# Turning the scaled keys in 32x32 blocks on VectorE and placing the blocks by DMA, in place of transposes on TensorE

## The chip, the core and the metric

The kernel runs on one core of a Trainium2 chip. A core has a matrix engine (TensorE, "PE" in the profile, with its weight loads as "PEld"), three elementwise engines (VectorE "DVE", ScalarE "ACT", GpSimd "POOL"), a queue engine that here does nothing but issue DMA transfers (SyncE, "SP"), and 16 DMA engines that move the data. Each engine runs its own instructions in the order in which they stand in the program; engines wait for one another only by semaphores. The metric is the device time of one execution in microseconds: before the change 647.9 us, the median of three runs (647.87 to 648.56).

## The reference

```python
def _attn_ref(r, k, v, w, u):                    # batch 4, heads 8, tokens 768, head size 48
    for t in range(S):
        cur = einsum('bhd,bhe->bhde', u * k[t], v[t])
        y[t] = einsum('bhd,bhde->bhe', r[t], state + cur)
        state = w[t] * state + einsum('bhd,bhe->bhde', k[t], v[t])

x = attn_out.transpose(0, 2, 1, 3).reshape(3072, 384)
h = x @ w_in                                     # 384 x 2048
out = (h * sigmoid(h)) @ w_out                   # 2048 x 384
```

A recurrence with a 48x48 state for each head and batch, whose rows decay by w at every token, and after it a two-layer network with SiLU between the layers. All is float32.

## The kernel before

**Units.** The work is cut in 12 units. A unit is one block of 128 tokens (six of them, n = 0 to 5) for two of the four batches, so unit i has n = i // 2. Units 0 and 1 take another path through the transposes (`i < NTOK`), and units 2 to 11 are alike. Of the two batches of a unit the second (b = 1) is kept with its tokens in reverse.

**Inside a unit.** Decays, queries and keys lie with channels on the partitions: `tw`, `tr` and `tk` hold for partition 64*e + d channel d of the even or odd head e of a pair, and along the free dimension rows of 128 tokens, one row for each head pair (NP = 4) and batch. Seven levels (l = 0 to 6) then build the scores of queries against keys in blocks of 1, 2, 4 ... 64 tokens. At each level TensorE makes the score products (line 527), VectorE keeps what the mask of the level allows (`keep_level`, line 537) and scales the queries (`grow_queries`, line 473, `prepare`, line 595), GpSimd scales the keys (`grow_keys`, line 491), and ScalarE copies. `burst` makes two levels of products in one go. `bonus_spread` and `bonus_write` (lines 440 to 452) put the term of u on the diagonal of the scores.

After level 6 the keys in `tk[:, NP:3*NP]` are scaled for the new state. The output is `y_state` (line 652, queries times the old state) plus `y` (line 665, scores times values), and `update` (line 679) adds keys times values to the decayed state. For `update` tokens have to lie on the partitions, since it sums over tokens; that is what `turn_k` is for: eight TensorE transposes of 128x128 (line 639, four for each batch) into PSUM, and a ScalarE copy of each batch's result to the tile `kq` (line 640). Units 10 and 11 hold the last tokens, and `update` returns at once for them (line 674), while `turn_k` is called for them too. `tk` has 16 rows: rows 4 to 11 are the keys, and rows 0 to 3 and 12 to 15 (`X = 0, NP + Q`) are scratch for the levels.

**The network.** `up(i, m)` (line 757, SiLU on line 763) makes a slice of the first layer for a whole unit, `quarter(i, x)` (line 820) seven products that give the second layer, with sums on VectorE (lines 802 and 829). Both lag behind the attention: while unit i is in its attention part, `quarter` of unit i - 2 and `up` of unit i - 1 are slipped in.

**What sets the order.** Nothing reorders the program (`manual_schedule`); it is written out by hand. For units 3 to 11 the loop at line 920 takes the groups of `mix(i)` one by one and puts after each of them the number of network steps that `ROOM` gives. Unit 2 is written out at lines 909 to 917. So on TensorE `turn_k` stands between two network steps near the unit's end, and `y_state`, `y` and `update` come after the last step of the unit, with the quarters of the next unit behind them.

**The DMA queue.** All loads and stores of units 2 to 11 are issued on SyncE's queue, in program order: per unit 48 loads of blocks of w, k and r for the unit after next (`load_blocks`, line 106, each 32 partitions x 8 rows x 32 or 16 values), five of v (lines 119 and 126), four of r and k for the bonus term (line 90), four that move the bonus sums (line 425), ten that move `yt` to `xt` (`move_x`, line 715) and two stores of the output (line 833).

Of the kernel before, what the change touches and what calls it, by code (L numbers as in the profile page):

```python
# [8 lines left out]
F32 = mybir.dt.float32  # L9
# [29 lines left out]
def kernel(  # L39
# [11 lines left out]
    nc = tc.nc  # L51

    B, H, S, D = r.shape
# [3 lines left out]
    NB = 2  # L57
    NP = H // 2
    PD = 64
    Q = NB * NP  # L60
    NX = Q + 2 * NP
    X = 0, NP + Q
# [3 lines left out]
    units = [(n, b0) for n in range(S // L) for b0 in range(0, B, NB)]  # L66
    NSLOT = 2
    NTOK = 2
# [4 lines left out]
    pt = ctx.enter_context(tc.tile_pool(name="pt", bufs=2))  # L73
    ps = ctx.enter_context(tc.tile_pool(name="ps", bufs=1, space=bass.MemoryType.PSUM))
# [174 lines left out]
    ident = const.tile([128, 128], F32, name="ident")  # L249
# [72 lines left out]
    tw, tr, tk, diag, kq, xt = {}, {}, {}, {}, {}, {}  # L322
# [297 lines left out]
    apart = {}  # L620
# [8 lines left out]
                                    ident[rows, rows])  # L629

    def turn_k(i, b):
        kq[i, b] = pt.tile([128, NP, 2 * PD], F32, name="kq")
        if i < NTOK:
            for e, have in enumerate(apart[i]):
                nc.scalar.copy(out=kq[i, b][:, :, PD * e:PD * e + D], in_=have[:, b])
            return
        p_tr = ps.tile([128, NP, 2 * PD], F32, name="p_m", bufs=2)
        for p in range(NP):
            nc.tensor.transpose(p_tr[:, p, :], tk[i][:, NP + (p, 2 * NP - 1 - p)[b], :], ident)  # L639
        nc.scalar.copy(out=kq[i, b], in_=p_tr)  # L640

    p_yt, p_kv, yt = {}, {}, {}

    def values(i, b):
        return vq[i] if b == 1 else vt[i]
# [25 lines left out]
    def update(i, b):  # L671
        n, b0 = units[i]
        if n == S // L - 1:
            return
        if b == 0:
            p_kv[i] = ps.tile([128, NB, NP, D], F32, name="p_m" if i < NTOK else "p_sc", bufs=2)
        for p in range(NP):
            for e in range(2):
                nc.tensor.matmul(p_kv[i][PD * e:PD * e + D, b, p, :], lhsT=kq[i, b][:, p, PD * e:PD * e + D],  # L679
                                 rhs=values(i, b)[:, 2 * p + e, :], start=(b == 0 and p == 0),  # L680
                                 stop=(b == NB - 1 and p == NP - 1))
        new = state[:, b0 + b]
        if n > 0:
            nc.gpsimd.tensor_tensor(out=new, in0=new,  # L684
                                    in1=tw[i][NL][:, b * NP:(b + 1) * NP, :].to_broadcast([128, NP, 2 * PD]),
                                    op=ALU.mult)
        if b < NB - 1:
            return
        for e in range(2):
            rows, cols = slice(PD * e, PD * e + D), slice(PD * e, PD * e + D)  # L690
            new = state[rows, b0:b0 + NB, :, cols]
            if n > 0:
                nc.vector.tensor_tensor(out=new, in0=p_kv[i][rows], in1=new, op=ALU.add)
            else:
                (nc.scalar.copy if i == 0 else nc.vector.tensor_copy)(out=new, in_=p_kv[i][rows])
# [23 lines left out]
    def both(fn, i, *args):  # L719
        return [(fn, i, b, *args) for b in range(NB)]  # L720

    def block_loads(i):
        return [(load_blocks, i, name, g) for name in "wkr" for g in range(4)]

    def mix(i):

        groups = [[*both(turn, i, "w"), (product, i, 0)],
                  [*both(turn, i, "k"), *both(turn, i, "r"), (odd_ones, i)], [(start_levels, i), (prepare_keys, i, 1)],
                  [(prepare, i, 1), *[(product, i, l) for l in range(1, NL)]],
                  [(burst, i, 1), (keep_level, i, 1)], [(keep_level, i, 2), (go_on, i, 2)],  # L730
                  [(prepare, i, 3), (reverse_v, i), (bonus, i, 0)],
                  [(burst, i, 3), (keep_level, i, 3), (bonus_sum, i, 0), (bonus, i, 1), (bonus, i, 2)],
                  [(keep_level, i, 4), (go_on, i, 4)],
                  [(prepare, i, 5), (bonus_sum, i, 1)] + ([(load_rk, i + 1)] if i + 1 < len(units) else []),
                  [(burst, i, 5), (keep_level, i, 5)], [(keep_level, i, 6), (go_on, i, 6), (bonus_spread, i), (bonus_write, i)],
                  both(turn_k, i), [*both(y_state, i), *both(y, i), *both(update, i), (move_x, i)]]

        loads = block_loads(i + NSLOT) if i + NSLOT < len(units) else []
        if i + 1 < len(units):
            loads.insert(len(loads) // 2, (load_values, i + 1))  # L740

        behind = groups[3 if i > NTOK + 1 else 10:]
        for at, group in enumerate(behind):
            group += loads[at * len(loads) // len(behind):(at + 1) * len(loads) // len(behind)]
        return groups
# [101 lines left out]
    def do(*steps):  # L847
        for fn, *args in steps:
            fn(*args)
# [20 lines left out]
    for l in range(1, NL):  # L870
        do((scores, 0, l), *[(grow_keys, 0, l + 1)] * (l + 1 < NL), *others[l])

    do((bonus, 1, 0), (bonus, 1, 1), (bonus, 1, 2), *both(y, 0), (turn_apart, 0), (join_weight, 0), (add_weight,),
       (product, 1, 0), (tail_weight, 1), (turn, 1, 0, "k"), (join_weight, 1), (dense_x, 0, 0), (turn, 1, 1, "k"),
       (dense_x, 0, 1), (grow_queries, 1, 0), (odd_ones, 1), (tail_weight, 2), *both(turn_k, 0), (head_weight, 2),
       (start_keys, 1, nc.gpsimd, True), (add_weight,), (up, 0, 0), (join_weight, 2), *blocks[4:8],
       (start_keys, 1, nc.gpsimd, False), (add_weight,), (tail_weight, 3), (odd_keys, 1, 1), (head_weight, 3), (grow_keys, 1, 1),
       (scores, 1, 1, (join_weight, 3)), (add_weight,), (up, 0, 1), (tail_weight, 4), (grow_keys, 1, 2), (head_weight, 4),
       (up, 0, 2))


    others = {1: blocks[8:12], 2: [(bonus_sum, 1, 0), (bonus_sum, 1, 1), (load_rk, 2), *both(update, 0)],
              3: [(bonus_spread, 1), (reverse_v, 1), (clear, 1), (load_values, 2)]}

# [4 lines left out]
    for m in range(1, 4):  # L889
# [3 lines left out]

    do((scores, 1, NL - 1), (join_weight, 8), (add_weight,), (up, 0, 7), *both(y, 1), (turn_apart, 1),
       (tail_weight, 9), *both(turn_k, 1), (dense_x, 1, 0), (head_weight, 9, [0]), (dense_x, 1, 1), (head_weight, 9, [1]),
       (join_weight, 9), (add_weight,), (tail_weight, 10), (head_weight, 10), *both(update, 1), (up, 1, 0), *both(turn, 2, "w"))
    blocks = block_loads(3)

# [5 lines left out]
    for m in range(6):  # L904
# [7 lines left out]
    do(blocks[2], (burst, 2, 3), (keep_level, 2, 3), (keep_level, 2, 4), (go_on, 2, 4), (prepare, 2, 5), (bonus, 2, 1),  # L912
       (bonus, 2, 2), (down, 0, 1, 2), (bonus_sum, 2, 1), (load_rk, 3), (sums, 1, 1), *blocks[3:7], (down, 0, 1, 3))
    do((burst, 2, 5), (keep_level, 2, 5), (keep_level, 2, 6), (go_on, 2, 6), (up, 1, 6), (bonus_spread, 2), (bonus_write, 2),
       (load_values, 3), *both(turn_k, 2), (weight_sums, 2), (up, 1, 7), (sums, 1, 2))
    do((sums, 1, 3), *both(y_state, 2), *both(y, 2), *both(update, 2), (move_x, 2),
       *blocks[7:])

    ROOM = 1, 1, 0, 2, 1, 1, 1, 1, 1, 2, 1, 2, 1, 0
    for i in range(3, len(units)):  # L920
        steps = downs(i - 2) + ups(i - 1)
        groups = mix(i)
        if i == NTOK + 1:

            groups[4].insert(1, (weight_sums, 3))
        for group, room in zip(groups, ROOM):
            do(*group)
            for step in steps[:room]:
                do(*step)
            steps = steps[room:]  # L930
# [32 lines left out]
```

## Time and profile before

| what | before |
|---|---|
| time, median of 3 | 647.9 us |
| span of the profiled run | 646.2 us |
| TensorE busy | 639.6 us |
| VectorE busy | 433.9 us |
| GpSimd busy | 283.1 us |
| ScalarE busy | 203.8 us |
| mean DMA rate | 76 GB/s |
| granted TensorE clock, mean | 1.000 |
| `turn_k`: transposes on line 639 | 80, 0.87 us for each eight on the chain |
| `turn_k`: copies on line 640 | 20, median 581 ns |

The busy times say how much an engine has to do in all. What sets the time is the chain of work that ended last: the profile follows it back from the last instruction, at each step to what released it. Of one unit in the middle of the run the engines' timelines and SyncE's own list of DMA issues tell how far each engine is ahead of the chain. In that list a transfer stands with the time that its issue occupied the queue; the time from issue to landing stands apart.

### The profile page before, as it was taken

How to read it: one execution, taken by the hardware profiler on the slowest of the kernel's cores; microseconds unless marked ns; L12 is line 12 of the kernel's file. 1: busy time of each engine (PE TensorE's matmuls, PEld its weight loads, DVE VectorE, ACT ScalarE, POOL GpSimd, SP SyncE). 2: the span in 40 equal slices, each digit the busy share in tenths (PEclk: the TensorE clock that was granted, in tenths of full speed). 3: DMA queues.
4: the chain of work that ended last, by engine and by line, in shares of the span. 5: the costliest groups of instructions: out<-in, count | busy, mean ns of one | idle time of the engine just before them, and what ended most of it. 6: DMA issues, size and time to landing. Idle time of an engine off the chain costs nothing.

```text
span 646.2 us, 12889 instructions
## 1 busy us (share of the span) xinstructions
PE 639.6 (99%) x4878; PEld 579.2 (90%) x4878; DVE 433.9 (67%) x737; ACT 203.8 (32%) x408; POOL 283.1 (44%) x356
## 2 busy tenths in 40 slices
PE   8999999999999999999999999999999999999998
PEld 7888876898899899899899899899899989989997
DVE  7879789896777677586586586676586766751031
ACT  5798872212321321320321231231232232131120
POOL 6898398466065054254334425416416505510000
PEclk9999999999999999999999999999999999999999
DMA  9975954433534524513513513423432022000000
GB/s 229 276 180 131 229 129 50 91 75 52 96 63 69 96 49 72 88 31 64 98 29 67 96 28 58 96 37 52 90 54 38 26 50 50 27 2 25 25 0 25
DMA packets 201134, 49.21 MB, mean 76 GB/s; under 512 B 188912, under 2 KB 195952, under 8 KB 201072
## 3 DMA queue, kind: packets, MB, share of 16 engines
q1 hardware_dynamic: 199488, 47.79, 36.5%
q10 hardware_dynamic: 1584, 0.59, 0.4%
q8 instruction: 39, 0.64, 0.4%
q14 instruction: 23, 0.19, 0.1%
HBM read 39.52 MB, written 4.72 MB: 68 GB/s over the span
## 4 chain that ended last, share of the span: by engine, by line
PE 95%; DVE 2%; POOL 1%; ACT 1%; issue 1%; POOLq 0%; DVEq 0%; ACTq 0%
PE p_h L757 39%; PE p_o L820 31%; PE p_sc L527 6%; PE p_m L527 4%; PE p_m L776 3%; PE p_m L665 3%; PE p_m L652 3%; PE p_m L639 1%; PE p_sc L679 1%; POOL tk L491 1%; PE p_m L350 1%; PE p_m L855 1%; PE p_m L703 0%; DVE score L450 0%; POOL w_in_sb L227 0%
## 5 line engine op out<-in xcount | busy, mean ns | idle before, releaser
L757 PE MATMUL p_h<-xt,w_in_sb 128*128 128x256 f32 x1152 | 258.4, 382 | 0.7 <-POOL tk L507 0.7
L757 PEld LDWEIGHTS p_h<-xt,w_in_sb 128*128 128x128 f32 x1152 | 215.8, 190 | 32.5 <-POOL tk L507 0.9
L763 ACT ACTIVATE gt<-p_h 128x512 f32<-128x512 f32 x93 | 55.5, 596 | 228.2 <-PE p_h L757 228.1
L491 POOL TENSOR_TENSOR tk<-tk,tw 128x256 f32<-128x256 f32 x144 | 102.1, 732 | 23.3 <-ACT tk L461 16.6
L537 DVE COPY_PREDICATED score<-mask,p_sc 128x512 f32<-128x512 int8 x78 | 64.1, 885 | 59.7 <-PE p_sc L527 59.4
L820 PE MATMUL p_o<-own,temps 128*128 128x192 f32 x528 | 90.3, 328 | 0.4 <-DVE temps L829 0.4
L820 PE MATMUL p_o<-w_out_sb,gt 128*128 128x192 f32 x528 | 90.4, 328 | 0.0
L820 PEld LDWEIGHTS p_o<-own,temps 128*128 128x128 f32 x528 | 85.8, 190 | 1.8 <-DVE temps L829 0.7
L820 PEld LDWEIGHTS p_o<-w_out_sb,gt 128*128 128x128 f32 x528 | 85.9, 190 | 0.9 <-issue 0.4
L684 POOL TENSOR_TENSOR state<-state,tw 128x512 f32<-128x512 f32 x16 | 19.3, 1225 | 118.5 <-PE p_m L652 118.5
L386 POOL TENSOR_TENSOR tw<-tw 128x256 f32<-128x256 f32 (+6 forms) x83 | 39.8, 480 | 54.5 <-DVE tw L338 50.6
L802 DVE TENSOR_TENSOR temps<-gt 128x256 f32<-128x256 f32 x88 | 44.3, 504 | 21.9 <-ACT gt L763 21.9
L461 ACT COPY tk<-tk 128x256 f32<-128x256 f32 x60 | 24.6, 410 | 83.4 <-PE p_sc L527 40.8
L527 PEld LDWEIGHTS p_sc<-tr,tk 48*128 48x128 f32 x640 | 39.2, 186 | 12.1 <-issue 8.9
L473 DVE TENSOR_TENSOR tr<-tr,tw 128x512 f32<-128x512 f32 x53 | 46.0, 868 | 3.3 <-POOL tk L491 1.0
L527 PE MATMUL p_sc<-tr,tk 48*128 48x128 f32 x640 | 47.1, 285 | 0.6 <-POOL tk L491 0.6
L408 POOL TENSOR_TENSOR ruk<-tokens_rk 128x768 f32<-128x768 f32 x10 | 18.6, 1858 | 65.8 <-DVE own_sums L415 65.8
L595 DVE TENSOR_TENSOR tr<-tr,tw 128x512 f32<-128x512 f32 x29 | 39.9, 1375 | 1.3
L537 DVE COPY_PREDICATED score<-mask,p_m 128x512 f32<-128x512 int8 x54 | 35.4, 706 | 0.0
L820 PE MATMUL p_o<-w_out_sb,temps 128*128 128x192 f32 x176 | 30.4, 326 | 0.0
L829 DVE TENSOR_TENSOR partial<-p_o,partial 128x192 f32<-128x192 f32 x33 | 11.6, 353 | 27.6 <-PE p_o L820 27.6
L597 ACT COPY tr<-tr 128x512 f32<-128x512 f32 x29 | 18.4, 634 | 35.8 <-DVE tr L473 35.0
(144 smaller groups left out, 753.3 us busy)
## 6 DMA issues: line engine op xcount, KB each, us to landing
w_out_sb<-in_moe_w_in_dram SPq DMA_DIRECT2D x6, 768.0 KB, 6.9
tokens_rk<-in_r_dram SPq DMA_DIRECT2D x20, 192.0 KB, 3.4
tokens_rk<-in_k_dram SPq DMA_DIRECT2D x20, 192.0 KB, 3.8
w_out_sb<-in_moe_w_out_dram SPq DMA_DIRECT2D x4, 768.0 KB, 6.3
own<-in_moe_w_out_dram SPq DMA_DIRECT2D x4, 768.0 KB, 5.8
xt<-yt SPq DMA_DIRECT2D x60, 48.0 KB, 2.0
raw<-in_w_dram SPq DMA_DIRECT2D x80, 32.0 KB, 2.2
raw<-in_k_dram SPq DMA_DIRECT2D x80, 32.0 KB, 2.4
```

Of the source, the lines that this page charges most:

```text
L386: engine.tensor_tensor(out=up, in0=t[:, :, 0::2], in1=t[:, :, 1::2], op=ALU.mult)
L461: nc.scalar.copy(out=keys(i, X[(l + 1) % 2] * L + c, [4 * c, blocks], [c, 2], [1, c]), in_=keys(i, NP * L + c, [4 * c, blocks], [NP * L + ...
L473: nc.vector.tensor_tensor(out=odd, in0=odd, in1=tw[i][l][:, :, 0::2][:, :, :, None].to_broadcast([128, Q, L >> (l + 1), c]), op=ALU.mult)
L491: nc.gpsimd.tensor_tensor(out=out, in0=have, in1=odd_products(i, l, b, *blocks), op=ALU.mult)
L527: nc.tensor.matmul(bass.AP(tensor=s_p.tensor, offset=s_p.offset, ap=[s_p.ap[0], [apart * L // 2, 2], [1, L // 2]]), lhsT=tk[i][rows, X[l % ...
L537: nc.vector.copy_predicated(out=dst, mask=masks[l][:, :, None].to_broadcast([128, NB, NP, ni, c]), data=sc[e].rearrange("p (b q) (i c) -> ...
L595: nc.vector.tensor_tensor(out=new[:, :, :, 1, :], in0=old[:, :, :, 1, :], in1=tw[i][l][:, :, 0::2][:, :, :, None].to_broadcast([128, Q, L ...
L652: nc.tensor.matmul(p_yt[i, b][:, p, :], lhsT=state[:, b0 + b, p, :], rhs=tr[i][:, b * NP + p, :], start=(p == 0), stop=False)
L757: nc.tensor.matmul(p_h[:, a, :], lhsT=w_in_sb[:, c, f * 128:(f + 1) * 128], rhs=xt[i][:, c, :], start=(c == 0), stop=(c == KC - 1))
L763: nc.scalar.activation(out=gt[i, m], in_=p_h, func=AF.Silu)
L802: nc.vector.tensor_tensor(out=out, in0=one, in1=two, op=op)
L820: nc.tensor.matmul(p, lhsT=left(f), rhs=right[:, f, :], start=(f == 0), stop=(f == FH - 1))
```

## The change

The transposes leave TensorE. For units 2 to 9 `turn_blocks` has VectorE turn the scaled keys in blocks of 32x32, one instruction of 128x512 for each batch, into the scratch rows of `tk`; a block then lies on the partitions of its channels, and its place in `kq` is on the partitions of its tokens. So 32 DMA transfers (2 halves of a head's channels x 2 heads of a pair x 4 groups of tokens x 2 batches) move the blocks to `kq`. `kq` becomes one tile for both batches, with one buffer. Units 10 and 11 turn no keys. Units 0 and 1 keep their path, with the new shape of `kq`. In `mix` the group with `turn_k` falls away, `turn_blocks` goes to the end of the group before it, and `ROOM` gives this group the three network steps of both.

```diff
     def turn_k(i, b):
-        kq[i, b] = pt.tile([128, NP, 2 * PD], F32, name="kq")
-        if i < NTOK:
-            for e, have in enumerate(apart[i]):
-                nc.scalar.copy(out=kq[i, b][:, :, PD * e:PD * e + D], in_=have[:, b])
-            return
-        p_tr = ps.tile([128, NP, 2 * PD], F32, name="p_m", bufs=2)
-        for p in range(NP):
-            nc.tensor.transpose(p_tr[:, p, :], tk[i][:, NP + (p, 2 * NP - 1 - p)[b], :], ident)
-        nc.scalar.copy(out=kq[i, b], in_=p_tr)
+        if b == 0:
+            kq[i] = pt.tile([128, NB, NP, 2 * PD], F32, name="kq", bufs=1)
+        for e, have in enumerate(apart[i]):
+            nc.scalar.copy(out=kq[i][:, b, :, PD * e:PD * e + D], in_=have[:, b])
+
+    def turn_blocks(i):
+
+        kq[i] = pt.tile([128, NB, NP, 2 * PD], F32, name="kq", bufs=1)
+        for b in range(NB):
+            nc.vector.transpose(out=tk[i][:, X[b]:X[b] + NP, :], in_=tk[i][:, NP + b * NP:2 * NP + b * NP, :])
+        for a in range(2):
+            width = min(D - 32 * a, 32)
+            for e in range(2):
+                t = tk[i][(2 * e + a) * 32:(2 * e + a + 1) * 32]
+                for g in range(4):
+                    for b in range(NB):
+                        nc.sync.dma_start(out=kq[i][g * 32:(g + 1) * 32, b, :, PD * e + 32 * a:PD * e + 32 * a + width],
+                                          in_=t[:, X[b]:X[b] + NP, g * 32:g * 32 + width])
...
+        back = b == 1 and i >= NTOK
         for p in range(NP):
             for e in range(2):
-                nc.tensor.matmul(p_kv[i][PD * e:PD * e + D, b, p, :], lhsT=kq[i, b][:, p, PD * e:PD * e + D],
+                nc.tensor.matmul(p_kv[i][PD * e:PD * e + D, b, p, :], lhsT=kq[i][:, b, NP - 1 - p if back else p, PD * e:PD * e + D],
...
-                  [(burst, i, 5), (keep_level, i, 5)], [(keep_level, i, 6), (go_on, i, 6), (bonus_spread, i), (bonus_write, i)],
-                  both(turn_k, i), [*both(y_state, i), *both(y, i), *both(update, i), (move_x, i)]]
+                  [(burst, i, 5), (keep_level, i, 5)],
+                  [(keep_level, i, 6), (go_on, i, 6), (bonus_spread, i), (bonus_write, i), *[(turn_blocks, i)] * (i < len(units) - NB)],
+                  [*both(y_state, i), *both(y, i), *both(update, i), (move_x, i)]]
...
-       (load_values, 3), *both(turn_k, 2), (weight_sums, 2), (up, 1, 7), (sums, 1, 2))
+       (load_values, 3), (turn_blocks, 2), (weight_sums, 2), (up, 1, 7), (sums, 1, 2))
...
-    ROOM = 1, 1, 0, 2, 1, 1, 1, 1, 1, 2, 1, 2, 1, 0
+    ROOM = 1, 1, 0, 2, 1, 1, 1, 1, 1, 2, 1, 3, 0
```

## The prediction

> **What bounds the kernel now.** I read the page's first part, then the chain that ended last in order of time, cut to one unit (unit 6), then VectorE's timeline and SyncE's issues over the same microseconds.
>
> ```profile
> PE 639.6 (99%) x4878; PEld 579.2 (90%) x4878; DVE 433.9 (67%) x737; ACT 203.8 (32%) x408; POOL 283.1 (44%) x356
> ```
>
> TensorE is busy for all but 1% of the span. The chain (start, us, engine, tile and line) shows that it is also what everything ends on: start follows start without a gap.
>
> ```profile
> 315.75 0.89 PE p_m L527 x16
> 316.64 7.97 PE p_h L757 x36
> 324.61 0.87 PE p_m L639 x8
> 325.48 2.59 PE p_h L757 x12
> 328.07 1.78 PE p_m L652 x16
> 329.86 1.88 PE p_m L665 x32
> 331.74 0.72 PE p_sc L679 x32
> 332.46 10.60 PE p_o L820 x64
> ...
> 366.69 0.89 PE p_m L527 x16
> 367.58 7.97 PE p_h L757 x36
> ```
>
> The last products of scores end at 316.64; call this moment E. The eight transposes take 0.87 us of the chain, and `update` (L679) begins at E + 15.10. From its end at 332.46 to the next unit's E at 367.58 are 35.12 us, and a unit takes 50.94.
>
> VectorE's timeline tells when the new turning could begin: the last write of scores ends at 323.75, E + 7.1. The turning of the raw keys, the same instruction and shape, takes 669 ns.
>
> ```profile
> 321.25 2.50 DVE L450 COPY_PREDICATED score<-own_mask,both_b 128x1024 f32<-128x1024 int8 x2
> ...
> L338 DVE STREAM_TRANSPOSE tk<-raw x20: 667/669/705, 78.8 to 535.8; 128x512 f32<-128x512 f32 x20
> ```
>
> SyncE's issues (start, us, line, transfer, count) are the view that decides. Eight loads of blocks take 3.90 us of the queue, 0.49 each, whether a run is 128 or 64 bytes; ten moves from SBUF to SBUF 6.29, 0.63 each, and four of the smaller ones 2.44, 0.61 each.
>
> ```profile
> 310.75 2.44 SPq L425 DMA_DIRECT2D diag<-own_sums  x4
> ...
> 320.17 3.90 SPq L106 DMA_DIRECT2D raw<-in_r_dram  x8
> 332.40 6.29 SPq L715 DMA_DIRECT2D xt<-yt  x10
> ```
>
> The page gives 2.0 us from issue to landing for such a move:
>
> ```profile
> xt<-yt SPq DMA_DIRECT2D x60, 48.0 KB, 2.0
> ```
>
> **What the Trainium skill says.** "Perfetto Trace Analysis", section What "DMA-bound" means, counts as one of its bounds the issuing engine's sequencer when its track is solid DMA slices, since that window is descriptor generation and not data movement. The trace agrees: the issues lie end to end at a fixed price, while the DMA engines are busy 36% in this unit (windows view).
>
> "VectorE: DVE Perf Modes", section The three transpose paths: VectorE turns blocks of 32x32 only, not a full 128x128. So the blocks must be carried to other partitions, which is what the 32 transfers are; the trace confirms the price of the turning alone.
>
> "TensorE: Matmul & The Clock Gate", section Part 1: after an idle window of about 3.4 us the array runs at half rate until it has been busy about as long. The record of the granted clock shows 1.00 throughout, but the warming matmuls agree: the first sixteen took 3.68 us, sixteen of the same a little later 1.97.
>
> ```profile
> 1.36 3.68 PE L855 MATMUL p_m<-ident 128*128 128x128 f32 x16 [1.36 <-POOL ident masks.py:199]
> ...
> 11.70 1.97 PE L855 MATMUL p_m<-ident 128*128 128x128 f32 x16
> ```
>
> **Removed.** Eight transposes in each of ten units: 10 x 0.87 = 8.7 us of the chain. Twenty ScalarE copies of 581 ns: ScalarE is busy 32% and waits for TensorE, so nothing. With the two last units nothing comes in their place, so there 2 x 0.87 = 1.7 us is a clear gain.
>
> **Added on VectorE.** Two turnings a unit, 2 x 0.67 = 1.34 us, from E + 7.1 to E + 8.45. Behind them stand the sums of line 802, which the second layer needs about 10 us later, in its third product, and VectorE is busy 35 of the 50.94 us. GpSimd has scaled the keys long before, since its queue is idle from 313.2. Nothing for VectorE, then, except as the start of what follows.
>
> **Added on SyncE.** 32 transfers a unit. No row shows exactly this shape, so I bound it: below by the block loads, 0.49 us (also 32 partitions and three dimensions, but from HBM), above by a little over the moves to `xt`, 0.65. I take 0.61, the small SBUF moves, because these also begin and end in SBUF. That the DMA engines keep up is seen at 316 to 324: 16 loads, 4096 packets of at most 128 bytes, at a busy share of 0.61 (windows view), and 32 blocks are again 4096 packets, over more than twice the time.
>
> The first transfer waits for the first turning, the second for the second, at E + 8.45. The thirty after it come at 0.61: the last is issued at E + 8.45 + 18.3 = E + 26.75 and lands 2.0 later, at E + 28.75.
>
> **The new wait.** `update` sums over all tokens, so each of its matmuls needs all four token groups and both halves of the channels of its head: the first batch's set ends with the next to last transfer. On TensorE `update` stands before the next unit's quarters, and the engine keeps order. Without the transposes it would be reached at E + 15.10 - 0.87 = E + 14.2. So TensorE stands still for 28.75 - 14.2 = 14.5 us, and `update` comes 28.75 - 15.10 = 13.65 us later than before. Nothing gives this back: the state, the next turning of w, k and r on VectorE and the quarters all stand behind it. With 0.49 and a landing of 2.2 (the block loads) it is 8.45 + 14.7 + 2.2 - 15.10 = 10.25; with 0.65 and 2.5, 15.35.
>
> **Unit 2 is worse off,** since there SyncE is already late:
>
> ```profile
> 132.64 2.15 SPq L126 DMA_DIRECT2D vq<-in_v_dram  x4
> 134.90 6.56 SPq L715 DMA_DIRECT2D xt<-yt  x10
> ```
>
> Its transfers come after these loads of v and ahead of the moves to `xt`, so at 134.9, though the blocks would be turned at about 126. The last lands at 134.9 + 31 x 0.61 + 2.0 = 155.8; `update` of unit 2 began at 127.2. That is 28.6 us (24.9 to 30.4).
>
> **Does the queue keep up later?** In a steady unit 73 other issues (48 loads x 0.49, ten xt x 0.63, the rest) are some 38 us of queue between the last block of one unit and the first of the next. From that last block's issue to the next turned keys TensorE needs 2.0 + 0.72 + 35.12 + 1.7 + 8.45 = 48 us. It keeps up. Only before unit 4 are there 98 issues (loads of unit 3 move behind its blocks), 51 us: 3 us more.
>
> **Cold clock.** Each of the eight stalls is far over 3.4 us. I take 3.68 - 1.97 = 1.7 us each from the start of the trace, 13.6 in all; ends 0 and 3.4 (two windows lost at half rate).
>
> **Sum.** 28.6 + 7 x 13.65 + 3 + 13.6 - 1.7 = 139.0. Forecast: 647.9 + 139 = 787 us.
>
> **Rivals.**
> *The placing is hidden, and the transposes are a gain.* For: before, SyncE is idle from 324.07 to 332.40, just where the blocks come, and TensorE is the bound. Against: hiding 32 issues before E + 14.2 allows (14.2 - 2.0 - 8.45) / 30 = 0.125 us each, and no transfer in SyncE's list comes near. It would give 647.9 - 8.7 = 639 us.
> *The stall is there but short,* because an SBUF block issues in 0.31 us, the least that any block load took. Then a steady unit is 8.45 + 9.3 + 2.0 - 15.10 = 4.65 later, unit 2 134.9 + 9.6 + 2.0 - 127.2 = 19.3; with 13.6 for the clock and 1.7 off: 647.9 + 7 x 4.65 + 19.3 + 13.6 - 1.7 = 712 us. Against: the median of the loads is 449 ns, and no move between SBUF tiles went under 522.
> *SyncE becomes the bound outright,* if a block costs over 0.9 us by a slow path for its three dimensions: each unit then adds 8.45 + 27 + 2.0 - 15.1 = 22.4, and unit 2 37.6: 647.9 + 7 x 22.4 + 37.6 + 13.6 - 1.7 = 854 us. Nothing in the profile speaks for it but that the shape is new.
>
> **How the numbers follow.** Forecast 0.78, hidden 0.05, short stall 0.11, slow path 0.06. The ends of the forecast: 24.9 + 7 x 10.25 + 3 - 1.7 = 98, so 746 with no cold clock; 30.4 + 7 x 15.35 + 3 + 27.2 - 1.7 = 166, so 814. To have 8 in 10 I go a little towards the short stall and past the top: 737 to 820. Faster is the hidden case alone, 0.05; for a result within 0.2% a stall would have to cancel the gain to a microsecond, 0.01; slower 0.94.
>
> **What would show it.** In the profile after: TensorE idle for about 14 us a unit ahead of the `update` matmuls, eight times, the first about twice as long, released by the DMA of `kq`; 32 issues of `kq` in a row on SyncE, about 0.6 us apart, the first right after VectorE's turnings of 0.67 us; a unit period near 66 us, against 50 for the last two; matmuls at double time for some microseconds after each stall. Wrong it would be if the issues come closer together than 0.4 us, or if matmuls after the stall keep their speed.

## The result, and the profile after

After the change the kernel takes 804.5 us (median of four runs, 803.0 to 805.45) against 648.1 us before on the same chip (647.87 to 648.56): the ratio is 1.241, with an interval of 1.2395 to 1.243. The change costs 156.4 us. The forecast was 787 us, with a range of 737 to 820.

The first part of the page after has TensorE busy for only 82% of the span of 802.4 us. In the second part the clock row now has gaps, where it showed full speed throughout before. The fourth part, the chain, has SyncE's queue as the second largest holder.

```profile
PE 655.4 (82%) x4798; PEld 591.3 (74%) x4798; DVE 439.1 (55%) x753; ACT 193.8 (24%) x388; POOL 285.2 (36%) x356
...
PEclk9999997599779959987995997899699699999999
...
PE 72%; SPq 17%; DVE 3%; POOL 2%; issue 2%; DMA 2%; ACT 1%; POOLq 0%; ACTq 0%
```

The same two rows before:

```profile
PEclk9999999999999999999999999999999999999999
...
PE 95%; DVE 2%; POOL 1%; ACT 1%; issue 1%; POOLq 0%; DVEq 0%; ACTq 0%
```

The chain of unit 6, in order of time (start, us, what), answers to the one shown of before. E, the end of the last products of scores, is 405.71 here.

```profile
405.71 7.98 PE p_h L768 x36
413.71 0.61 ACT gt L774
414.32 0.54 SPq L648
...
433.21 0.59 SPq L648
...
433.85 1.77 DMA kq<-tk
...
435.76 1.49 PE p_sc L689 x30
437.25 12.14 PE p_o L831 x64
449.39 1.11 PE p_sc L527 x16
```

Before, the chain ran through TensorE from E to `update` without leaving it. Now it leaves TensorE at E + 8, goes through SyncE's queue one issue at a time for 19.5 us, and comes back at 435.76, E + 30.05. What follows is slower as well: `update` takes 1.49 us instead of 0.72, and the first quarters take 12.14 us instead of 10.60.

SyncE's list and TensorE's timeline over the same microseconds show both sides of the wait. The brackets hold the idle time before an instruction and what ended it.

```profile
413.44 21.65 SPq L648 DMA_DIRECT2D kq<-tk  x32
```

```profile
430.62 0.36 PE L689 MATMUL p_sc<-vt,kq 128*48 128x48 f32 x2 [10.69 <-DMA kq<-tk]
435.76 0.77 PE L689 MATMUL p_sc<-vt,kq 128*48 128x48 f32 x13 [4.77 <-DMA kq<-tk]
```

32 issues follow one another for 21.65 us, 0.68 each. TensorE stands still from 419.9 (430.62 - 10.69) to 435.76, but for two matmuls of an even head, whose blocks are issued ahead of the odd head's and have all landed.

The table of stretches gives the granted clock of the same stall. Its columns are the stretch, its length, then busy time and count of TensorE, of its weight loads, of VectorE, ScalarE and GpSimd, then the clock, the DMA share and GB/s.

```profile
421.00:425.00 4.00, 0.00 (x0) 0.00 (x0) 0.54 (x2) 0.00 (x0) 0.00 (x0) 0.78 0.16 24
425.00:429.00 4.00, 0.00 (x0) 0.00 (x0) 0.00 (x0) 0.00 (x0) 0.00 (x0) 0.50 0.13 15
...
435.70:439.70 4.00, 3.94 (x38) 3.88 (x39) 2.32 (x4) 0.00 (x0) 0.00 (x0) 0.50 0.31 53
439.70:443.70 4.00, 4.00 (x25) 4.00 (x24) 2.47 (x5) 0.98 (x2) 3.27 (x5) 0.92 0.19 49
```

A mean of 0.78 over four microseconds is 2.2 us at full speed and then half, so the clock fell at about 423.2, 3.3 us into the stall. It came back at about 440.3, 4.6 us after work had begun again. Over the eight stalls the trace's clock record has the fall 2.6 to 3.8 us into the stall and the return 3.2 to 5.3 us after the work. All changes in this record lie whole multiples of 3.41 us apart, so each of these times also depends on how the stall lies to these steps. While the blocks are being placed, hardly anything is computed and the DMA engines are busy 0.13 to 0.16: nothing is short of bandwidth.

The 156.4 us can be put together from the start times of `update` in the two chains:

| part | later than before, us | forecast, us |
|---|---|---|
| unit 2 (127.34 before, 155.59 after) | 28.3 | 28.6 |
| units 3 and 5 to 9, growth of each over its period before | 16.8, 16.1, 17.2, 16.6, 17.3, 17.4: sum 101.4 | 6 x 15.35 = 92.1 |
| unit 4 | 25.6 | 15.35 + 3 = 18.35 |
| after the last `update`: its cold clock, less the transposes of the two last units | 0.9, the rest of the spans' difference of 156.2 | 1.7 - 1.7 = 0 |
| sum | 156.2 | 139.0 |

(15.35 is the forecast's 13.65 for the stall and 1.7 for the clock.)

Unit 4 is the one that doesn't follow the others. SyncE's list (it ends at 285, so it has ten of the 32), ScalarE's timeline and TensorE's timeline before its stall:

```profile
267.11 2.44 SPq L425 DMA_DIRECT2D diag<-own_sums  x4
...
276.54 1.93 SPq L106 DMA_DIRECT2D raw<-in_r_dram  x4
278.56 6.64 SPq L648 DMA_DIRECT2D kq<-tk  x10
```

```profile
269.53 0.20 ACT L441 COPY both_b<-diag 128x16 f32<-128x16 f32 x1 [3.83 <-DMA diag<-own_sums]
```

```profile
272.17 4.54 PE L768 MATMUL p_h<-xt,w_in_sb 128*128 128x256 f32 x12 [1.93 <-ACT gt L774]
```

E of this unit is 262.3. SyncE reaches the blocks at E + 16.3, where it was at E + 7.7 in unit 6. The 98 issues since the blocks of unit 3 took it from 223.4 to 278.6, 55.2 us, and it waited for nothing in between. The moves of the bonus sums, which stand in the same queue, are late as well: ScalarE waits 3.83 us for them before its SiLU, and TensorE 1.93 us for ScalarE. This second stall, ahead of the first, adds nothing to the time here: VectorE's turnings end at 275.6, SyncE comes to the blocks only at 278.6, straight from its loads, and `update` begins when they have landed, at 300.6. The whole delay of unit 4 is the queue's.

### The profile page after: what moved, and what is told of

Same layout as the page of the kernel before. It is cut to its first block, busy times and chain, and to the rows that moved or that the text cites. A ratio compares the mean times of both kernels' runs of the same rounds, so it can differ in the third digit from the quotient of the medians.

```text
span 802.4 us, 13027 instructions
## 1 busy us (share of the span) xinstructions
PE 655.4 (82%) x4798; PEld 591.3 (74%) x4798; DVE 439.1 (55%) x753; ACT 193.8 (24%) x388; POOL 285.2 (36%) x356
## 4 chain that ended last, share of the span: by engine, by line
PE 72%; SPq 17%; DVE 3%; POOL 2%; issue 2%; DMA 2%; ACT 1%; POOLq 0%; ACTq 0%
PE p_h L768 30%; PE p_o L831 27%; SPq L648 16%; PE p_sc L527 5%; PE p_m L527 3%; PE p_m L787 2%; DMA kq<-tk 2%; PE p_sc L689 2%; PE p_m L661 1%; PE p_m L674 1%; POOL tk L491 1%; DVE score L450 1%; PE p_m L350 0%; SPq L126 0%; DVE temps L813 0%
## 5 line engine op out<-in xcount | busy, mean ns | idle before, releaser
L689 PE MATMUL p_sc<-vt,kq 128*48 128x48 f32 x128 | 9.8, 284 | 138.8 <-DMA kq<-tk 138.8
L491 POOL TENSOR_TENSOR tk<-tk,tw 128x256 f32<-128x256 f32 x144 | 106.7, 764 | 28.1 <-ACT tk L461 21.3
L689 PEld LDWEIGHTS p_sc<-vt,kq 128*48 128x48 f32 x128 | 7.6, 187 | 141.8 <-issue 111.0
L831 PE MATMUL p_o<-w_out_sb,gt 128*128 128x192 f32 x528 | 103.2, 358 | 0.0
L831 PEld LDWEIGHTS p_o<-w_out_sb,gt 128*128 128x128 f32 x528 | 98.6, 213 | 1.1 <-issue 0.4
L703 DVE TENSOR_TENSOR state<-p_sc,state 48x384 f32<-48x384 f32 x16 | 8.9, 555 | 138.3 <-PE p_sc L689 138.2
L838 ACT COPY partial<-p_o 128x192 f32<-128x192 f32 x11 | 3.5, 319 | 190.8 <-PE p_o L831 190.8
L473 DVE TENSOR_TENSOR tr<-tr,tw 128x512 f32<-128x512 f32 x53 | 43.8, 826 | 3.3 <-POOL tk L491 1.0
L595 DVE TENSOR_TENSOR tr<-tr,tw 128x512 f32<-128x512 f32 x29 | 38.5, 1326 | 1.3
```

The source lines that it names most:

```text
L473: nc.vector.tensor_tensor(out=odd, in0=odd, in1=tw[i][l][:, :, 0::2][:, :, :, None].to_broadcast([128, Q, L >> (l + 1), c]), op=ALU.mult)
L491: nc.gpsimd.tensor_tensor(out=out, in0=have, in1=odd_products(i, l, b, *blocks), op=ALU.mult)
L595: nc.vector.tensor_tensor(out=new[:, :, :, 1, :], in0=old[:, :, :, 1, :], in1=tw[i][l][:, :, 0::2][:, :, :, None].to_broadcast([128, Q, L ...
L831: nc.tensor.matmul(p, lhsT=left(f), rhs=right[:, f, :], start=(f == 0), stop=(f == FH - 1))
```

## The experiments

The theory: all of the loss is SyncE's queue, at a fixed price for each issue, with TensorE waiting in order behind `update`; the cold clock comes on top. The rivals: VectorE's turnings delay the levels; the DMA engines or their small packets are the limit; the time belongs to the clock.

**1. The turnings without the transfers.** VectorE turns as after; the 32 transfers are left out, and `kq` is set to zero once and reused, so in units 2 to 9 the state gets nothing added.

```diff
-        kq[i] = pt.tile([128, NB, NP, 2 * PD], F32, name="kq", bufs=1)
+        if i == NTOK:
+            kq[i] = pt.tile([128, NB, NP, 2 * PD], F32, name="kq", bufs=1)
+            nc.gpsimd.memset(kq[i], 0.0)
+        else:
+            kq[i] = kq[NTOK]
...
-                        nc.sync.dma_start(out=kq[i][g * 32:(g + 1) * 32, b, :, PD * e + 32 * a:PD * e + 32 * a + width],
-                                          in_=t[:, X[b]:X[b] + NP, g * 32:g * 32 + width])
```

> Leaves out the 32 transfers of each unit: kq is cleared once and never filled, so update adds nothing to the state; the turnings on VectorE and all else of the change stay. Queue theory (the whole loss is the issuing of the transfers on SyncE and the wait for them): the loss goes and the gain of the removed transposes shows, 647.9 - 8.7 = 639 us. Rival, VectorE's turnings delay what stands behind them: over 650 us.

Measured: 640.75 us (640.58 to 640.92), ratio 0.988 (0.985 to 0.991). The first part of its page:

```profile
PE 631.1 (99%) x4798; PEld 570.7 (89%) x4798; DVE 439.7 (69%) x753; ACT 193.3 (30%) x388; POOL 283.3 (44%) x357
```

TensorE is the bound again, and VectorE is as busy as after the change (439.1) at no cost to the span. Without the transfers the removed transposes bring 7.8 us of the 8.7 forecast. So the turnings don't hold TensorE up, and the transfers, with what waits for them, account for the whole loss: 804.5 - 640.75 = 164 us.

**2. The same bytes in 16 transfers.** The turned keys of both batches go to adjacent rows, and one transfer takes 8 rows in place of 4.

```diff
-            nc.vector.transpose(out=tk[i][:, X[b]:X[b] + NP, :], in_=tk[i][:, NP + b * NP:2 * NP + b * NP, :])
+            nc.vector.transpose(out=tk[i][:, b * NP:b * NP + NP, :], in_=tk[i][:, NP + b * NP:2 * NP + b * NP, :])
...
-                    for b in range(NB):
-                        nc.sync.dma_start(out=kq[i][g * 32:(g + 1) * 32, b, :, PD * e + 32 * a:PD * e + 32 * a + width],
-                                          in_=t[:, X[b]:X[b] + NP, g * 32:g * 32 + width])
+                    nc.sync.dma_start(out=kq[i].rearrange("p b q d -> p (b q) d")[g * 32:(g + 1) * 32, :, PD * e + 32 * a:PD * e + 32 * a + width],
+                                      in_=t[:, 0:2 * NP, g * 32:g * 32 + width])
```

> Same bytes and same number of packets in 16 transfers a unit instead of 32 (both batches in one). Queue theory, 0.67 us for each issue whatever it carries: 16 x 0.67 = 10.7 us less in each of the eight stalls, 804.5 - 86 = 719 us, or 712 if the 7 us lost to the late bonus sums in one unit go too. Rival, the DMA engines need the time for 4096 short packets: no change, about 800 us.

Measured: 728.1 us (726.86 to 729.33), ratio 1.123 (1.118 to 1.128). SyncE's list of unit 6:

```profile
376.35 10.56 SPq L647 DMA_DIRECT2D kq<-tk  x16
```

An issue with twice the bytes and twice the runs takes 0.66 us, as before, and half as many give back 76 of the 156 us. Between these two sizes the price is for the issue, not for what it carries. The time is 9 us above the expectation: by the start times of `update` a stall is 7.9 to 10.3 us shorter, where 10.7 was expected. The clock still falls in the stalls (mean 0.946).

**3. Half of the 32 on ScalarE's queue.** The blocks of the first batch stay with SyncE, those of the second are issued by ScalarE after the unit's last network step.

```diff
-                    for b in range(NB):
-                        nc.sync.dma_start(...
+                    queue.dma_start(...
...
+                  [... (turn_blocks, i), (place_blocks, i, 0, nc.sync)],
+                  [(place_blocks, i, 1, nc.scalar), *both(y_state, i), *both(y, i), *both(update, i), (move_x, i)]]
```

> Again 32 transfers with the same packets, but those of the second batch are issued on ScalarE's queue, behind the SiLU of the unit's last network step. Queue theory: the halves run side by side, SyncE's done at E + 19, ScalarE's begin at about E + 11.5 and land at E + 24 instead of E + 30, so 6 to 8 us less in each stall, about 745 us. Rival, the DMA engines are the limit: no change, about 800 us.

Measured: 777.9 us (776.0 to 779.8), ratio 1.200 (1.193 to 1.207). ScalarE's timeline, SyncE's list and SyncE's waits from 395 to 420:

```profile
404.27 10.79 ACTq L650 DMA_DIRECT2D kq<-tk  x16
```

```profile
407.46 10.69 SPq L650 DMA_DIRECT2D kq<-tk  x16
```

```profile
SPq L650 <- DMA kq<-tk: 7.6, 2, 7.3
```

For 7.6 us both queues issue at once, and neither gets slower: 0.67 us each. So the DMA engines are not the limit either. But the gain is small, since SyncE's first issue waits 7.3 us for the landing of a key transfer, and only ScalarE has any under way then. The queues run in parallel, but the program's waits tie one to the other's completions. In the whole run SyncE's first issue waits so six times, 43.8 us in all. I read it as completion semaphores that both queues share; no run separates this from another cause, though experiment 8 speaks against a dependence on the data, since there the wait goes when GpSimd takes ScalarE's place.

"DMA: Bandwidth & Descriptors" of the Trainium skill, section Issuing engines are not separate DMA queues, says that transfers from all issuing engines run on the same 16 DMA engines, so several issuers save only the issue time, which is "usually small relative to the DMA itself". That several issuers save issue time agrees with this run; that the transfers run on the same engines no run here shows. That the issue time is small doesn't fit this case: a landing takes 1.8 us, but 32 issues one after the other take 21.65.

**4. TensorE kept busy through the stall.** To price the clock, 60 matmuls whose result nobody reads (115 in unit 2) stand ahead of `update`.

```diff
+    def fill(n):
+        p = ps.tile([128, L], F32, name="p_m", bufs=2)
+        for x in range(n):
+            nc.tensor.matmul(p, lhsT=ident, rhs=ident, start=True, stop=True)
...
-                  [*both(y_state, i), *both(y, i), *both(update, i), (move_x, i)]]
+                  [*both(y_state, i), *both(y, i), *[(fill, 60)] * (i < len(units) - NB), *both(update, i), (move_x, i)]]
```

> The changed kernel, with matmuls on the identity in front of update, 60 a unit (about 13 us) and 115 in unit 2 (25 us), that nobody reads: they fill most of each stall. Cold clock theory: matmuls keep their speed after the stall, which saves the 2.3 us that the quarters and update took longer, eight times: about 786 us. Rival, matmuls after the stall are slow because the transfers and the state work share SBUF with them: no change, 804 us.

Measured: 805.9 us (805.0 to 806.8), ratio 1.243 (1.239 to 1.247), no gain. TensorE's timeline and the table of stretches of unit 6:

```profile
439.24 0.48 PE L689 MATMUL p_sc<-vt,kq 128*48 128x48 f32 x13 [2.04 <-DMA kq<-tk]
```

```profile
440.00:442.00 2.00, 2.00 (x19) 1.91 (x16) 1.28 (x3) 0.00 (x0) 0.00 (x0) 0.50 0.40 54
```

The fill ended 2.04 us too early, and the clock fell to half although TensorE had stood still for no longer than that. In this run the pauses of 1.85 to 2.61 us ahead of `update` (units 3 and 5 to 8) were each followed by one step of 3.41 us at half clock, the pause of 1.50 us in unit 9 was not. Besides, `update` of unit 2 begins 2.3 us later than in the changed kernel, since SyncE comes to its blocks 1.1 us later and takes 1.2 us longer for the 32, and the later units keep this lag. The run doesn't decide on the price of the clock, so it was made again with 72 (132 in unit 2).

```diff
-*[(fill, 60)]
+*[(fill, 72)]
...
-(fill, 115)
+(fill, 132)
```

> The changed kernel with 72 unread matmuls on the identity in front of update instead of 60 (132 in unit 2), so that they last to the end of the stall. Cold clock theory: the granted clock stays at 1.00 and the slow matmuls go, 2.3 us a unit, while update may come up to 1 us later: 788 to 796 us. Rival, the slow matmuls cost nothing that the queue does not cost anyway: 804 us or more.

Measured: 801.5 us (801.1 to 802.0), ratio 1.2365 (1.234 to 1.239). Now the 64 matmuls of the quarters after the stall of unit 6 take 10.60 us again, from 438.82 to 449.42, and the clock stays at 1.00. So the slow matmuls come from standing still, and not from sharing SBUF with the transfers, which are the same here. The time lies between the two expectations: the three periods from unit 5 to unit 8 take 66.6 to 66.8 us in place of 67.6 to 68.2, and up to unit 7 `update` begins 0.3 to 3.4 us later than without the fill: SyncE's run in unit 2 is again late and long, by 0.9 us each, and in units 3, 6 and 7 the fill outlasts the blocks. So the 3 us gained are not the price of the clock. That stands in the chain: 2.3 us in unit 6, which for eight stalls would be some 18 of the 156 us (an estimate from this one unit).

**5. The two last units alone.** The kernel before, where units 10 and 11 turn no keys.

```diff
-                  both(turn_k, i), [*both(y_state, i), *both(y, i), *both(update, i), (move_x, i)]]
+                  both(turn_k, i) if i < len(units) - NB else [], [*both(y_state, i), *both(y, i), *both(update, i), (move_x, i)]]
```

> The kernel before with one edit: units 10 and 11 turn no keys. Sixteen transposes less on TensorE: 2 x 0.87 = 1.7 us, so 646.3 us. If what stands behind them set the pace there: no change.

Measured: 646.28 us (645.84 to 646.63, eight runs), ratio 0.9971 (0.9961 to 0.9981). The 1.7 us of the forecast are there, and this part is free of any price.

**6. `update` put off until the blocks have come.** 16 transfers, and `update` of unit i moved into the next unit, ahead of the burst of levels 3 and 4; its sums go to the PSUM tile `p_o` instead of `p_sc`.

```diff
-                  [(burst, i, 3), (keep_level, i, 3), (bonus_sum, i, 0), (bonus, i, 1), (bonus, i, 2)],
+                  [*both(update, i - 1), (burst, i, 3), (keep_level, i, 3), (bonus_sum, i, 0), (bonus, i, 1), (bonus, i, 2)],
...
-                  [*both(y_state, i), *both(y, i), *both(update, i), (move_x, i)]]
+                  [*both(y_state, i), *both(y, i), (move_x, i)]]
```

> 16 transfers a unit on SyncE, and update moved behind the quarters of the next unit, about 20 us later on TensorE. Theory that only the wait in front of update costs: no wait is left, 640 us. My theory adds the next wait in line: the scratch rows that the transfers read belong to tk, so the next unit's turning of k waits until they land, at E + 20.3 instead of E + 17.4, and the burst behind it has less slack than that, 1 to 3 us a unit: 650 to 665 us.

Measured: 696.0 us (694.7 to 698.1), ratio 1.074 (1.072 to 1.076): better than 728 us, but far from hidden. VectorE's timeline and TensorE's waits (in all, times, longest):

```profile
378.44 1.30 DVE L338 STREAM_TRANSPOSE tk<-raw 128x512 f32<-128x512 f32 x2 [5.65 <-DMA kq<-tk]
```

```profile
PE p_o L831 <- DVE temps L840: 33.5, 8, 14.7
```

TensorE no longer waits for the blocks, but VectorE does: the turned keys lie in `tk`, so the next unit's raw keys can't be turned into it before the transfers have read it. Behind that turning stand the sums that TensorE's quarters need. The wait has moved, as the longer estimate expected, but the time is 31 us above its upper end.

**7. The turned keys in a tile of their own.** They go to the room of `ruk`, which is free then, and `kq` is narrowed to make the two fit.

```diff
+        kt[i] = pt.tile([128, NB * NP, L], F32, name="ruk", bufs=1)
...
-            nc.vector.transpose(out=tk[i][:, b * NP:b * NP + NP, :], in_=tk[i][:, NP + b * NP:2 * NP + b * NP, :])
+            nc.vector.transpose(out=kt[i][:, b * NP:b * NP + NP, :], in_=tk[i][:, NP + b * NP:2 * NP + b * NP, :])
```

> As the run with update moved and 16 transfers, but the turned keys go to a tile of their own (in the room of the bonus products, with kq cut to 48 columns a head), so the next unit's keys need not wait for the transfers. Queue theory: no wait on TensorE; what is left is the load of SyncE's queue, 40 us of other issues and 16 x 0.66 in a unit of 50 us, so it may just bind: 640 to 648 us. If transfers beside the work cost by themselves, it stays over 655 us.

Measured: 672.1 us (671.95 to 673.52), ratio 1.0375 (1.036 to 1.039), above the expected 640 to 648. TensorE's longest wait, and the one of ScalarE behind it:

```profile
PE p_h L771 <- ACT gt L777: 20.3, 6, 10.4
```

```profile
ACT both_b L441 <- DMA diag<-own_sums: 31.6, 6, 12.3
```

The wait for blocks is gone from TensorE and VectorE. What is left is the queue as a whole: from 361.98 to 415.67, 53.7 us, SyncE issues without a break but for one wait of 0.7 us, and a unit of the kernel before takes 50.94. So the bonus sums, behind everything in the queue, come late to ScalarE, and TensorE waits for its SiLU, as in unit 4 of the changed kernel.

**8. Half of the 16 on another queue.** Two ways from there: the blocks of the odd heads go to ScalarE's queue, or to GpSimd's; those of the even heads stay with SyncE.

```diff
+(place_blocks, i, 0, nc.sync)
...
+(place_blocks, i, 1, nc.scalar)
```

> As before with the turned keys in a tile of their own, and half of the 16 transfers on ScalarE's queue, so that SyncE has 45 us of issues in a unit of 50. Queue theory: the gain of the removed transposes in full, 647.9 - 8.7 = 639, so 639 to 642 us, faster than the kernel before. Rival: ScalarE's issues hold up its copies, 645 us or more.

```diff
+(place_blocks, i, 0, nc.sync), (place_blocks, i, 1, nc.gpsimd)
```

> As the run with update moved, 16 transfers and the turned keys in a tile of their own, but eight of the 16 are issued on GpSimd's queue, which is idle at that place[...]. SyncE then has 53 - 8 x 0.66 = 47.7 us of issues in a unit of 50. Theory that SyncE's load is what is left: the bonus sums are in time, no wait on TensorE, 639 to 645 us, faster than before. Rival: GpSimd needs over 1 us for each issue and is late with the next unit's products, 650 us or more.

With ScalarE: 684.9 us (682.3 to 687.8), ratio 1.058 (1.056 to 1.061), worse than with SyncE alone. With GpSimd: 649.1 us (647.4 to 650.7, twelve runs), ratio 1.0016 (1.0005 to 1.0027). SyncE's waits with ScalarE, GpSimd's timeline with GpSimd, and the one long wait on TensorE there:

```profile
SPq L106 <- DMA kq<-ruk: 49.3, 22, 6.5
```

```profile
330.11 4.62 POOL L652 DMA_DIRECT2D kq<-ruk  x8 [11.86 <-DVE ruk L644]
```

```profile
227.16 4.51 PE L773 MATMUL p_h<-xt,w_in_sb 128*128 128x256 f32 x12 [6.33 <-ACT gt L779]
```

With ScalarE's queue SyncE's loads wait 49.3 us in all for the landing of blocks, the tie of experiment 3 again. The rival of the expectation isn't ruled out, though: ScalarE's `yt` copies stand behind its own issues and their waits, 43.2 us in seven times, and no run separates the two. GpSimd issues eight in 4.62 us, 0.58 each, and SyncE's loads have no such wait. One stall is left, 6.33 us in unit 4, again behind the bonus sums. It is why the time lies a little above the 639 to 645 expected.

**9. The bonus sums on GpSimd's queue too.** They are issued behind the keys of level 6.

```diff
+    def bonus_move(i):
...
-                nc.sync.dma_start(out=diag[i][b][s::2], in_=own_sums[b * L // 2:(b + 1) * L // 2, s])
+                nc.gpsimd.dma_start(out=diag[i][b][s::2], in_=own_sums[b * L // 2:(b + 1) * L // 2, s])
```

> The run with half of the 16 transfers on GpSimd's queue, and the four moves of the bonus sums go to that queue too, behind the keys of level 6. What was left there was one stall of 6.7 us in unit 4, where these moves came late in SyncE's queue and ScalarE waited for them ahead of its SiLU. Theory: that stall and the slow clock behind it go, 649.1 - 6.7 - 2 = 640 us, 639 to 643, faster than the kernel before. Rival: GpSimd's issues now come too late for the bonus itself, and every unit waits a little, 645 us or more.

Measured: 641.76 us (641.32 to 643.87, six runs), ratio 0.9915 (0.990 to 0.993): 0.85% faster than the kernel before. The first part of its page:

```profile
PE 632.3 (99%) x4798; PEld 570.8 (89%) x4798; DVE 431.6 (67%) x753; ACT 193.7 (30%) x388; POOL 341.2 (53%) x460
```

TensorE is the bound again, the granted clock of this run is 1.000, and no wait on TensorE is over 1.4 us. This is 1 us above the time of experiment 1, where the transfers were left out.

## Why the prediction was right, point by point

- **Removed, 8.7 us, of which 1.7 in the two last units.** Right: 7.8 us in experiment 1, 1.7 in experiment 5.
- **Nothing for VectorE.** Right by experiment 1. A turning takes a median of 682 ns where 667 to 669 was read off the raw keys.
- **32 issues in a row, `update` behind them, and nothing gives it back.** Right, and shown by experiments 1 and 2: without the transfers no loss, with half of the issues about half of it.
- **0.61 for an issue, the last landing at E + 28.75.** The size is off. An issue takes 0.60 us (median 599 ns) and about 0.05 passes to the next, as the chain shows; the 2.44 us for four issues, read as 0.61 each, hold only three of these passes. A run of 32 takes 21.1 to 21.7 us, 0.66 to 0.68 each; the longest, in unit 6, has one issue of 1.45 us, whose cause the profile doesn't tell. In unit 6 the second issue goes out at E + 8.6, about as forecast, and the landing takes 1.8. `update` waits only for the last block of the first batch, the 31st, though the sum took the 32nd. The 31st lands at E + 29.9, so `update` comes 14.95 us later than before, not 13.65. Over units 3 and 5 to 9 it is 14.3 to 14.95, 14.65 in the mean. The forecast's bounds of 10.25 and 15.35 hold this.
- **Unit 2, 28.6 us.** Measured 28.3, with the queue late where it was expected. That it agrees to 0.3 us is in part luck: SyncE comes to the blocks at 133.8, 1.1 us sooner than assumed, and the issues up to the 31st take about 1 us longer. (The lower end of 24.9 takes 2.0 us for the landing, where that of a steady unit takes 2.2; with 2.2 it is 25.1.)
- **Only before unit 4 ... 3 us more.** This step failed most: unit 4 took 25.6 - 15.35 = 10.3 more than the forecast's steady unit, or 8.7 more than a measured one (101.4 / 6 = 16.9). The price of the issues was too low here as well: the 98 took 55.2 us, 0.56 each, not 51, so SyncE came to the blocks at E + 16.3, where the forecast has E + 8.45 + 3 = E + 11.45. This is about 5 of the 7.3 us that unit 4 is over its forecast; the dearer run of 32 and the slower clock are the rest. The bonus sums, which stand behind the blocks in the same queue, were left out too. In the changed kernel their lateness is hidden under the stall; it costs time only once the stall is gone, in experiments 7 to 9.
- **Cold clock, 1.7 us for each stall.** Right in kind, by the clock row and by the fill of 72. The size is off: in unit 6 the slower `update` and quarters add 0.77 + 1.54 = 2.3 us, half of the 4.6 us for which work ran at half clock, and the sixteen matmuls from which 1.7 was read took only 3.68 us. (The clock record of before, read as 1.00 throughout, begins 6.5 us into the span, after those matmuls.) "TensorE: Matmul & The Clock Gate" of the Trainium skill, section Part 1, puts the idle window at about 3.4 us; in the eight stalls here the clock fell after 2.6 to 3.8. The pauses of 1.85 to 2.61 us with a fall behind them in experiment 4 are shorter than the page would have it.
- **The rivals.** The hidden case asks for 0.125 us an issue, the short stall for 0.31, the slow path for over 0.9; none of the 256 issues took less than 585 ns, and the median is 599.

The 17 us that the forecast lacks are thus 7.3 in unit 4, 9.3 in the six other steady units (1.55 each, about 1.0 of stall and the rest clock), and 0.9 at the end, less 0.3 in unit 2.

## What to carry to other kernels

When work of an engine is to be replaced by many small transfers, count the issues first: their number times the price of one on the issuing queue has to fit into the time between the data being ready and its first reader, and the queue's whole load into the period. Here 32 at 0.65 stood against a slack of 4 us. If it doesn't fit, merge transfers, put the reader later, give the data a tile that nothing else waits for, and use a queue that isn't tied to the first by its waits; then look at every other transfer behind them in the queue. The gain of the removed work comes only once all of these are done: here 728, 696, 672, 649 and at last 642 us.

## What the hardware showed that I had not expected

- Issues of key moves cost 0.60 to 0.61 us (medians) whether a row carries 32 or 16 values and whether 4 or 8 rows go, against a median of 0.449 for loads of blocks from HBM in the kernel before.
- GpSimd's queue issues such a move in 0.58 us, no slower than SyncE's 0.60.
- Two queues that issue at once don't slow each other: 0.67 us on each, where one alone took 0.66 to 0.68.
- TensorE's clock fell after pauses of 1.85 us and more, but not after one of 1.50 us (the kernel with 60 filling matmuls), and after the long stalls it came back 3.2 to 5.3 us after the work.
